# Score tiles of two heads in one TensorE tile: keys kept twice, key blocks not split over batches

## The chip, the cores and the metric

The kernel runs on one core of a Trainium2 chip. The metric is the device time of one execution in microseconds (us), before and after one change. The engines are TensorE (PE, with its weight loads shown as PEld), VectorE (DVE), ScalarE (ACT), GpSimd (POOL) and SyncE (SP), which only issues transfers here. Each engine works through its own queue in order and waits at semaphores for the others.

## What is computed

A parallel block: layer norm, then causal attention over a window of 256 tokens with 32 heads of 16 channels, and a gated bilinear feed-forward of width 1792, both added to the input. There are 2048 tokens of 512 channels; inputs and the output are bf16.

```python
xn = layernorm(x)                                   # x: (1, 2048, 512)
q, k, v = split(xn @ wqkv)                          # 32 heads, 16 channels each
scores = einsum("bhqd,bhkd->bhqk", q, k) * 16 ** -0.5
mask = (i - j >= 0) & (i - j < 256)                 # i: query, j: key
p = softmax(where(mask, scores, -1e9))
attention = merge_heads(einsum("bhqk,bhkd->bhqd", p, v)) @ wo
ffn = einsum("bsf,fd->bsd", (xn @ w_gate) * (xn @ w_up), w_down)
out = x + attention + ffn
```

## The kernel before

The tokens are cut into four chunks T of 512 tokens (eight blocks of 64), and the 32 heads into four groups c of eight heads. One of the 16 combinations (T, c) is called a pair; pairs run in the order of T and then c, and are numbered 0 to 15.

For a pair, the scores of keys against queries are taken in blocks of 64 keys by 64 queries. A query block q needs the key blocks q - 4 to q, so a pair of T 1 to 3 has 40 such blocks (each for eight heads) and a pair of T = 0 has 30. The function `layout` (L50) lists them by hand as batches of segments `(k, q, m, at)`: key block k (negative: of the chunk before) against m query blocks from q on, written at column block `at` of the score tile. A pair has five batches (four for T = 0), each up to eight column blocks wide. The eight heads of a group lie as four row strips of 32 partitions (index e); each strip holds two heads of 16 channels, called lanes. Keys are stored as K, and a second time as Ko, where the rows of the even head are set to zero (`i_odd`, L236). `i_scores` (L186) issues eight matmuls for a segment: for lane 0 16 rows of K, for lane 1 32 rows of Ko, each giving a tile of 64 keys by 64 m queries; lane 0 lands in PSUM partitions 0 to 63, lane 1 in 64 to 127, strip e in the e-th bank of the score tile S (four banks, one copy).

ScalarE takes the exponential of a whole batch from S into one of seven SBUF buffers P (L450). GpSimd then sets what the mask excludes to zero: `i_select` (L199, its instruction is L203) clears a triangle in diagonal blocks (q = k) and the other triangle in blocks q = k + 4. `selects` (L61) makes the list for one batch: it takes two blocks of the same kind into one instruction when their columns lie exactly four apart (a 64x512 select), and one alone otherwise (64x256); each is issued once per lane. The selects of one batch depend on each other in the planner's list. Then `i_values` (L206) multiplies with V, again eight matmuls for a segment, summed in two PSUM banks M; VectorE transposes, divides (L477, L486) and transposes back into OT.

PSUM has four more banks, M0 to M3, which the dense matmuls share (L184: q, k, gate, up, down, output projection; L595: v). VectorE and ScalarE evacuate them; on k this is `k_out` (L611).

The order of each engine's queue is made when the kernel is built, by a planner (`loop`, `choose`, `do`) that keeps estimated times of its own. A score batch can be placed once its keys, its queries, the score tile and a buffer P are free (`score_deps`); of seven buffers a pair holds five until its values are done, so at most two batches of the next pair can stand ahead of them. Batches are also kept at least `PACE` = 3.0 us apart in the planner's time. Values are placed when all selects of the pair should be done (`value_deps`); dense work fills the rest. Each operation carries the planner's estimate of its duration, such as 1.12 us for the values of a pair.

Of the kernel before, what the change touches and what calls it, by code (L numbers as in the profile page):

```python
# [8 lines left out]
F32 = mybir.dt.float32  # L9
I32 = mybir.dt.int32  # L10
ACT = mybir.ActivationFunctionType
ALU = mybir.AluOpType
# [37 lines left out]
def layout(T):  # L50


    ends = [(0, 4, 1, 0), (1, 5, 1, 1), (4, 4, 2, 2), (2, 6, 1, 4), (3, 7, 1, 5), (4, 6, 2, 6)]
    begins = [[(0, 0, 4, 0), (1, 1, 4, 4)], [(2, 2, 4, 0), (3, 3, 4, 4)]]
    if T == 0:
        return begins + [ends, [(5, 5, 3, 0), (7, 7, 1, 3), (6, 6, 2, 4)]]
    return [ends, [(-3, 0, 2, 0), (7, 7, 1, 2), (-2, 0, 3, 3), (6, 6, 2, 6)],
            [(-1, 0, 4, 0), (5, 5, 3, 4), (-4, 0, 1, 7)]] + begins
# [15 lines left out]
class Kernel:  # L74
# [11 lines left out]
    def open(self, ctx, tc, x, wqkv, wo, wg, wu, wd, out):  # L86
# [22 lines left out]
        self.K = some("K", 3, [128, 4, 512])  # L109
        self.Ko = some("Ko", 3, [128, 4, 512])  # L110
# [12 lines left out]
        self.odd = c.tile([128, 1], F32, name="odd")  # L123
# [4 lines left out]
    def prologue(self):  # L128
# [39 lines left out]
        nc.vector.tensor_copy(out=self.odd[:], in_=podd[:])  # L168
# [17 lines left out]
    def i_scores(self, T, c, batch):  # L186

        for k, q, m, at in batch:
            U, j = divmod(8 * T + k, 8)
            for lane in range(2):  # L190
                for e in range(4):
                    rows = slice(32 * e, 32 * e + (32 if lane else 16))
                    self.nc.tensor.matmul(  # L193
                        self.S[64 * lane:64 * lane + 64, e, 64 * at:64 * (at + m)],
                        lhsT=(self.Ko if lane else self.K)[U % 3][rows, c, 64 * j:64 * j + 64],
                        rhs=self.Q[T % 2][rows, c, 64 * q:64 * (q + m)],
                        start=True, stop=True, tile_position=(32 * e, 64 * lane), skip_group_check=True)
# [38 lines left out]
    def i_odd(self, T, c):  # L236
        self.nc.vector.tensor_scalar(out=self.Ko[T % 3][:, c, :], in0=self.K[T % 3][:, c, :],
                                     scalar1=self.odd[:, 0:1], scalar2=None, op0=ALU.mult)
# [186 lines left out]
    def score_deps(self, g):  # L425
        T, c, batch = self.batches[g]
        deps = {("S", g - 1), ("Pfree", g - self.PBUFS)}
        for k, q, m, at in batch:
            U, j = divmod(8 * T + k, 8)
            deps |= {("K", U, c, j // 2), ("Ko", U, c, j // 2), ("Q", T, c, q // 2), ("Q", T, c, (q + m - 1) // 2)}  # L430
# [30 lines left out]
    def do_values(self, at):  # L461
# [3 lines left out]
        o = self.pe(at, 1.12 if T else 0.86, f"V{v}")  # L465
# [57 lines left out]
    def first_chunk(self):  # L523
# [10 lines left out]
        first = []  # L534
        for b in range(4):
# [18 lines left out]
            def kq_out(o, i, b=b, tok=tok):  # L554
                x = self.op(f"K0b{b}", {"V": (0.21, 0.3)}, [o],
# [164 lines left out]
```

## Time and profile before

| | |
|---|---|
| time, median of 3 runs | 291.81 us (291.37 to 295.12) |
| time of the profiled execution | 291.58 us |
| its span, first to last instruction | 289.8 us |
| mean granted TensorE clock | 0.993 |
| instructions in the profile | 11641 |
| DMA traffic | 14.10 MB, mean 49 GB/s |

The 1.8 us between span and time lie outside the program's instructions. In the rows of the profile, "L203" is line 203 of the kernel; "P<-P" names what an instruction writes and reads; "64x512" is partitions by elements; "x208" is a count. In a group's row, the number after the bar is busy time in us, then the mean duration of one in ns, and after the second bar the idle time of the engine just before them with what ended it. In a row of a timeline the first two numbers are start and duration in us, and what stands in brackets is the idle time before it. In the chain in order of time they are the start of a piece and its length. In the table of windows there are, behind the window and its length, the busy times of PE, PEld, DVE, ACT and POOL with their counts, then the granted clock, the DMA share and GB/s.

### The profile page before, as it was taken

The page shows a single profiled execution, that of the slowest core. Times are in us where ns is not written, and L with a number is a line of the kernel's source. Part 1 is how long each engine was busy: PE and PEld are TensorE (multiplying, and loading weights), DVE is VectorE, ACT ScalarE, POOL GpSimd, SP SyncE. Part 2 cuts the span into 40 slices and gives each one's busy share as a digit, 9 for nine tenths or more (in the row PEclk, how much of TensorE's full clock was granted, in tenths as well). Part 3 has the DMA queues.
Part 4 walks back from the last instruction along what each step waited for, and adds up shares of the span by engine and source line. Part 5 has one row for each costly group of instructions (what it writes and reads, how often), then busy time and mean ns, then how long its engine had stood idle before and what let it go on. Part 6 is the DMA issues. An engine that isn't in the chain of part 4 may idle for free.

```text
span 289.8 us, 11641 instructions
## 1 busy us (share of the span) xinstructions
PE 271.8 (94%) x5296; PEld 138.5 (48%) x5296; DVE 185.0 (64%) x332; ACT 153.6 (53%) x98; POOL 175.5 (61%) x289
## 2 busy tenths in 40 slices
PE   6899999999999999798999899997997989989994
PEld 6564545665454545364454434546443444444541
DVE  7878987878954285767963466774614158658603
ACT  2057666567766656464856546652672735636000
POOL 3037695769868695658588664963657557484100
PEclk9999999999999999999999999999997999999999
DMA  7999310000041000000042000000000000000002
GB/s 228 374 370 351 81 20 2 3 5 2 2 76 38 23 20 3 2 2 5 0 78 57 20 2 2 2 3 5 2 18 23 18 23 2 1 5 2 2 0 72
DMA packets 17072, 14.10 MB, mean 49 GB/s; under 512 B 7040, under 2 KB 17024, under 8 KB 17024
## 3 DMA queue, kind: packets, MB, share of 16 engines
q1 hardware_dynamic: 16464, 12.85, 14.6%
q8 instruction: 41, 0.67, 1.0%
q10 hardware_dynamic: 560, 0.52, 0.6%
q14 instruction: 7, 0.06, 0.1%
HBM read 9.70 MB, written 2.10 MB: 41 GB/s over the span
## 4 chain that ended last, share of the span: by engine, by line
PE 81%; issue 7%; POOL 5%; DMA 2%; ACT 2%; SPq 1%; DVE 0%; ACTq 0%; POOLq 0%; DVEq 0%
PE M L184 60%; PE S L193 9%; PE M L213 7%; POOL P L203 5%; PE M L595 4%; DMA Wqkv<-in_A_wqkv_dram 2%; ACT P L450 2%; SPq L134 1%; DVE y L665 0%; DVE xnT L180 0%; DVE K L180 0%; ACTq L450 0%; POOLq L203 0%; DVEq L180 0%
## 5 line engine op out<-in xcount | busy, mean ns | idle before, releaser
L203 POOL TENSOR_SCALAR_AFFINE_SELECT P<-P 64x512 bf16<-64x512 bf16 (+1 forms) x272 | 169.0, 627 | 87.4 <-ACT P L450 75.5
L450 ACT ACTIVATE P<-S 128x2048 bf16<-128x2048 f32 x76 | 140.9, 1854 | 94.5 <-PE S L193 81.2
L184 PE MATMUL M<-xnT,Wg 128*128 128x512 bf16 x224 | 57.7, 380 | 0.0
L184 PE MATMUL M<-xnT,Wu 128*128 128x512 bf16 x224 | 57.7, 380 | 0.0
L184 PE MATMUL M<-Wd,hT 128*128 128x512 bf16 x224 | 54.7, 387 | 0.0
L644 DVE TENSOR_TENSOR hT<-M,gsb 128x512 bf16<-128x512 f32 x56 | 38.3, 683 | 12.9 <-PE M L184 12.4
L481 DVE STREAM_TRANSPOSE at<-M 128x512 f32<-128x512 f32 x32 | 21.4, 699 | 32.7 <-PE M L213 32.6
L213 PE MATMUL M<-P,V 64*17 64x64 bf16 (+3 forms) x2048 | 26.2, 228 | 9.7 <-POOL P L203 5.3
L180 DVE CAST gsb<-M 128x512 bf16<-128x512 f32 x43 | 29.5, 686 | 7.4 <-PE M L184 7.4
L193 PE MATMUL S<-Q,Ko 32*64 32x64 bf16 (+3 forms) x1024 | 34.2, 234 | 0.1
L193 PE MATMUL S<-Q,K 16*64 16x64 bf16 (+3 forms) x1024 | 33.8, 234 | 0.2 <-issue 0.2
L665 DVE TENSOR_TENSOR y<-M,x 128x512 bf16<-128x512 f32 x16 | 11.1, 692 | 35.8 <-PE M L184 35.6
L193 PEld LDWEIGHTS <-K 16*64 16x64 bf16 x1024 | 18.3, 104 | 31.9 <-issue 31.0
L184 PEld LDWEIGHTS <-hT 128*128 128x128 bf16 x224 | 20.3, 99 | 25.6 <-issue 4.3
L184 PEld LDWEIGHTS <-Wu 128*128 128x128 bf16 x224 | 20.5, 98 | 25.1 <-issue 2.2
L184 PE MATMUL M<-xnT,Wqkv 128*128 128x512 bf16 (+1 forms) x152 | 30.6, 346 | 2.1 <-DMA Wqkv<-in_A_wqkv_dram 0.9
L184 PEld LDWEIGHTS <-Wg 128*128 128x128 bf16 x224 | 20.0, 98 | 24.2 <-issue 2.0
L213 PEld LDWEIGHTS <-V 64*17 64x17 bf16 x2048 | 20.8, 84 | 13.3 <-issue 11.8
L184 PEld LDWEIGHTS <-Wqkv 128*128 128x128 bf16 x152 | 12.8, 98 | 15.7 <-issue 2.6
L193 PEld LDWEIGHTS <-Ko 32*64 32x64 bf16 x1024 | 17.7, 104 | 0.2 <-issue 0.2
L595 PE MATMUL M<-Wqkv,xnT 128*64 128x256 bf16 x256 | 15.5, 274 | 0.7 <-ACT xnT L178 0.7
L184 PE MATMUL M<-Wo,OT 128*128 128x512 bf16 x64 | 16.1, 379 | 0.0
(39 smaller groups left out, 143.9 us busy)
## 6 DMA issues: line engine op xcount, KB each, us to landing
out_dram<-y SPq DMA_DIRECT2D x16, 128.0 KB, 1.7
Wg<-in_B_w_gate_dram SPq DMA_DIRECT2D x2, 896.0 KB, 10.3
Wu<-in_B_w_up_dram SPq DMA_DIRECT2D x2, 896.0 KB, 11.9
Wd<-in_B_w_down_dram SPq DMA_DIRECT2D x1, 1792.0 KB, 17.6
Wqkv<-in_A_wqkv_dram SPq DMA_DIRECT2D x2, 512.0 KB, 6.4
x<-in_A_x_dram SPq DMA_DIRECT2D x1, 1024.0 KB, 13.5
x<-in_A_x_dram SPq DMA_DIRECT2D x1, 512.0 KB, 11.9
Wo<-in_A_wo_dram SPq DMA_DIRECT2D x1, 512.0 KB, 13.6
```

Source lines behind the costliest of these rows:

```text
L134: eng.dma_start(out=dst, in_=src)
L180: self.nc.vector.tensor_copy(out=out, in_=in_)
L184: self.nc.tensor.matmul(ps, lhsT=a, rhs=b, start=first and n == 0, stop=last and n == len(pairs) - 1)
L193: self.nc.tensor.matmul(self.S[64 * lane:64 * lane + 64, e, 64 * at:64 * (at + m)], lhsT=(self.Ko if lane else self.K)[U % 3][rows, c, 64 ...
L203: self.nc.gpsimd.affine_select(out=v, in_=v, pattern=[[0, 4], [0, n], [sign, 64]], base=0, fill=0.0, compare_op=ALU.is_gt if kind else ALU ...
L213: self.nc.tensor.matmul(banks[lane][32 * e:32 * e + 17, 64 * q:64 * (q + m)], lhsT=self.V[U % 3][rows, j, 4 * c + e, 0:17], rhs=P[rows, e, ...
L450: ex = self.op(f"exp{g}", {"A": (took + 0.06, took + 0.18)}, [o], lambda e: self.nc.scalar.activation(out=P[:, :, 0:hi], in_=self.S[:, :, ...
L481: t = self.op(f"tr{v}", {"V": (0.63, 0.71)}, [o] + ts, lambda e, par=par: nc.vector.transpose(out=self.at[:, :, par, :], in_=self.M[banks[ ...
L595: self.nc.tensor.matmul(self.M[i][64 * lane:64 * lane + 64, 256 * jj:256 * jj + 256], lhsT=self.xnT[T % 2][:, k, tok], rhs=w[:, lane], sta ...
L644: x = self.op(f"u{T}.{f}", {"V": PSUM_COPY["V"]}, [o, ("gate", T, f)], lambda e: self.nc.vector.tensor_tensor(out=self.hT[T % 2][:, f, :], ...
L665: self.nc.vector.tensor_tensor(out=keep["y"][:], in0=self.M[i][:], in1=self.x[:, t, :], op=ALU.add)
```

## The change

Keys are stored in one tile of shape [128, 4, 8, 2, 64]: for each group and key block two lanes of 64 keys, lane 0 with the odd head's rows zero, lane 1 with the even head's. One matmul with 32 rows and 128 key columns then gives the scores of both heads of a strip, so a segment takes four score matmuls. Each evacuation of keys becomes two operations that read the PSUM bank one after the other and multiply by a column of ones and zeros (`own`); the copy from K to Ko is gone.

The table in `layout` is new as well: a key block's segment, up to five query blocks, is never split over two batches. A pair has 12 segments in place of 17 (T = 0: 9 in place of 13), in as many batches. The planner's estimate for the values of a pair is raised.

```diff
 def layout(T):
-    ends = [(0, 4, 1, 0), (1, 5, 1, 1), (4, 4, 2, 2), (2, 6, 1, 4), (3, 7, 1, 5), (4, 6, 2, 6)]
...
-    return [ends, [(-3, 0, 2, 0), (7, 7, 1, 2), (-2, 0, 3, 3), (6, 6, 2, 6)],
...
+    return [[(3, 3, 5, 0), (-3, 0, 2, 5), (-4, 0, 1, 7)], [(2, 2, 5, 0), (6, 6, 2, 5), (7, 7, 1, 7)],
...
-        self.K = some("K", 3, [128, 4, 512])
-        self.Ko = some("Ko", 3, [128, 4, 512])
+        self.K = some("K", 3, [128, 4, 8, 2, 64])
...
-            for lane in range(2):
-                for e in range(4):
-                    rows = slice(32 * e, 32 * e + (32 if lane else 16))
-                    self.nc.tensor.matmul(
-                        self.S[64 * lane:64 * lane + 64, e, 64 * at:64 * (at + m)],
-                        lhsT=(self.Ko if lane else self.K)[U % 3][rows, c, 64 * j:64 * j + 64],
-                        rhs=self.Q[T % 2][rows, c, 64 * q:64 * (q + m)],
-                        start=True, stop=True, tile_position=(32 * e, 64 * lane), skip_group_check=True)
+            for e in range(4):
+                rows = slice(32 * e, 32 * e + 32)
+                self.nc.tensor.matmul(
+                    self.S[:, e, 64 * at:64 * (at + m)],
+                    lhsT=self.K[U % 3][rows, c, j].rearrange("p l t -> p (l t)"),
+                    rhs=self.Q[T % 2][rows, c, 64 * q:64 * (q + m)],
+                    start=True, stop=True, tile_position=(32 * e, 0), skip_group_check=True)
...
-    def i_odd(self, T, c):
-        self.nc.vector.tensor_scalar(out=self.Ko[T % 3][:, c, :], in0=self.K[T % 3][:, c, :],
-                                     scalar1=self.odd[:, 0:1], scalar2=None, op0=ALU.mult)
+    def i_keys(self, e, T, c, lane, in_, blocks=slice(0, 8)):
+
+        out, in_ = self.K[T % 3][:, c, blocks, lane, :], in_.rearrange("p (j t) -> p j t", t=64)
+        own = self.own[:, lane:lane + 1]
+        if e == "A":
+            self.nc.scalar.activation(out=out, in_=in_, func=ACT.Copy, scale=own)
+        else:
+            self.nc.vector.tensor_scalar(out=out, in0=in_, scalar1=own, scalar2=None, op0=ALU.mult)
...
-        o = self.pe(at, 1.12 if T else 0.86, f"V{v}")
+        o = self.pe(at, 1.42 if T else 1.12, f"V{v}")
...
         def k_out(o, i):
-            x = self.op(f"K{T}.{c}", PSUM_COPY, [o], lambda e: self.copy(e, self.K[T % 3][:, c, :], self.M[i][:]), rank=1)
+            x = o
+            for lane in range(2):
+                x = self.op(f"K{T}.{c}", PSUM_COPY, [o, x], lambda e, lane=lane: self.i_keys(
+                    e, T, c, lane, self.M[i][:]), rank=1)
             self.frees(x, i)
-            y = self.op(f"Ko{T}.{c}", {"V": (0.31, 0.44)}, [x], lambda e: self.i_odd(T, c), rank=4)
             for b in range(4):
-                self.at_["K", T, c, b], self.at_["Ko", T, c, b] = x, y
+                self.at_["K", T, c, b] = x
```

`selects` and `i_select` are not touched, but their lists follow from the table. GpSimd's queue at the start of a pair of chunk 3, before (pair 12: its first batch in buffer P_87, the next in P_88; "4x64" is one block for the four strips, "8x64" two blocks):

```order
L203 AFFINE_SELECT P_87<-P_87 64x4x64 [waits Activation_49]
L203 AFFINE_SELECT P_87<-P_87 64x4x64 [waits PE_49]
L203 AFFINE_SELECT P_87<-P_87 64x8x64 [waits PE_49,Pool_49] x2
L203 AFFINE_SELECT P_87<-P_87 64x8x64 x2
L203 AFFINE_SELECT P_88<-P_88 64x8x64 [waits Activation_49]
L203 AFFINE_SELECT P_88<-P_88 64x8x64 [waits PE_49]
```

and now (pair 13: its first batch in P_89, the next in P_90):

```order
L201 AFFINE_SELECT P_89<-P_89 64x4x64 [waits Activation_49]
L201 AFFINE_SELECT P_89<-P_89 64x4x64 [waits PE_49,Pool_49]
L201 AFFINE_SELECT P_89<-P_89 64x4x64 [waits Pool_49] x2
L201 AFFINE_SELECT P_89<-P_89 64x4x64 [waits PE_49] x2
L201 AFFINE_SELECT P_89<-P_89 64x4x64 [waits Pool_49]
L201 AFFINE_SELECT P_90<-P_90 64x4x64 [waits Activation_49]
```

The first batch of a pair had two one-block and four two-block selects; it now has eight one-block selects, the last of which stands behind the first select of the next batch.

The planner also orders TensorE's queue anew. At the values of pair 11, the last of chunk 2, before (scores of pair 12's first batch, then the first values):

```order
L193 LDWEIGHTS Ko_75
L193 MATMUL S<-Q_71,Ko_75 64x128
L213 LDWEIGHTS V_80
L213 MATMUL M_110<-P_89,V_80 17x64 [waits Pool_49]
L213 LDWEIGHTS V_80
L213 MATMUL M_110<-P_89,V_80 17x64
```

now, first the last dense matmuls ahead of these values (the up projection of chunk 2) and the first values,

```order
L183 LDWEIGHTS Wu
L183 MATMUL M_106<-xnT_78,Wu 128x512
L211 LDWEIGHTS V_77 [waits DVE_49]
L211 MATMUL M_107<-P_86,V_77 17x320 [waits Pool_49]
L211 LDWEIGHTS V_77
L211 MATMUL M_107<-P_86,V_77 17x320
```

and at their end the last values and the first matmuls behind them, for the keys of chunk 3 (then come its queries and a first part of its values, and then the scores of pair 12):

```order
L211 LDWEIGHTS V_77
L211 MATMUL M_108<-P_90,V_77 17x256
L183 LDWEIGHTS Wqkv [waits DMAHW2_49,DMAHW3_49,DMAHW1_49,DMAHW0_49]
L183 MATMUL M_109<-xnT_79,Wqkv 128x512 [waits DVE_49]
L183 LDWEIGHTS Wqkv
L183 MATMUL M_109<-xnT_79,Wqkv 128x512
```

The scores of pair 12's first batch, with the keys, queries and first values of chunk 3, have moved from ahead of pair 11's values to behind them. Between the scores of pair 12's last batch and those of pair 13's first there stand 52 dense matmuls now.

25 lines of the change are left out of this document (11 added, 14 removed).

## The prediction

> **What bounds the kernel now.** I read the page's list of engines first, then the chain that ended last, then the list of waits, then the chain in order of time.
>
> ```profile
> PE 271.8 (94%) x5296; PEld 138.5 (48%) x5296; DVE 185.0 (64%) x332; ACT 153.6 (53%) x98; POOL 175.5 (61%) x289
> PE 81%; issue 7%; POOL 5%; DMA 2%; ACT 2%; SPq 1%; DVE 0%; ACTq 0%; POOLq 0%; DVEq 0%
> PE M L213 <- POOL P L203: 5.3, 3, 2.1
> PE M L213 <- issue: 4.4, 3, 1.7
> ```
>
> TensorE (PE) sets the pace, and nearly its only waits are in the value matmuls of line 213, for the selects of GpSimd (POOL, line 203): 5.3 + 4.4 = 9.7 us. GpSimd has 114 us to spare. The next rows, the chain in order of time, show one pair: a batch of scores (S, L193), twelve dense matmuls (M, L184), and so on, then the values (M, L213).
>
> ```profile
> 104.78 0.35 PE S L193 x16
> 105.14 2.69 PE M L184 x12
> 107.83 0.35 PE S L193 x16
> 108.19 2.69 PE M L184 x12
> 110.88 0.53 PE S L193 x48
> 111.41 2.70 PE M L184 x12
> 114.11 0.36 PE S L193 x32
> 114.47 1.50 PE M L213 x121
> 115.97 1.47 issue
> ...
> 270.47 1.44 PE M L213 x123
> 271.90 14.15 PE M L184 x65
> 286.08 0.69 DVE y L665
> ```
>
> Dense matmuls come every 14.15 / 65 = 0.217 us. From 104.78 to 107.83 are 3.05 us with twelve of them (2.60), so a batch of 16 score matmuls costs 0.45 us. A batch of 48 takes 0.53 where 16 take 0.35 and 32 take 0.36: the matmuls of a batch overlap, and only the six-segment batch pays for its number of instructions.
>
> **The change on TensorE.** Segments fall from 17 to 12 in a pair (13 to 9 in token chunk 0), the score matmuls of a segment from eight to four. A batch now has two or three segments; the streamed columns are the same. So a batch costs 0.35 to 0.36, and what goes is the six-segment batch's 0.53 - 0.35 = 0.18, once in each of 16 pairs: 2.9 us. Values: 0.18 for four extra segments is 0.045 for one; some five fewer are 0.2 us for each of 16 pairs, 3.2 us (bounds: nothing, since the columns stay, and 5/17 of 1.44 us, 6.8 in all; I take 3.2, since short segments are what the score row prices). Together 6.1 us of TensorE time. Loads of 32x128 weights have no row. The nearest:
>
> ```profile
> 104.71 0.11 PEld L193 LDWEIGHTS <-K 16*64 16x64 bf16 x4 [0.42 <-issue]
> L184 PEld LDWEIGHTS <-Wu 128*128 128x128 bf16 x224 | 20.5, 98 | 25.1 <-issue 2.2
> ```
>
> Four loads of 64 columns take 0.11 us together, and one of 128 columns 0.098. So four of 128 lie between 0.11 (no change, which I take, since a full load is no longer than a small one) and twice that, some 0.25 us a batch, 1.8 us over the seven batches of steps 3 and 4 below.
>
> **The change on GpSimd.** It follows from the layout, and no line of the select itself changes. A select takes two blocks in one instruction only where they lie four columns of the table apart. The old table was laid out for that: a pair of chunks 1 to 3 has 14 two-block and 4 one-block selects (chunk 0: 10 and 4). In the new table segments of 5 and 3 put the diagonals five columns apart: 32 one-block selects a pair (chunk 0: 20, and 2 two-block). All in all 272 become 472.
>
> ```profile
> L203 POOL TENSOR_SCALAR_AFFINE_SELECT P<-P 64x512 bf16<-64x512 bf16 x208 | 139.8, 678 | 44.0 <-ACT P L450 34.3
> L203 POOL TENSOR_SCALAR_AFFINE_SELECT P<-P 64x256 bf16<-64x256 bf16 x64 | 29.5, 462 | 43.4 <-ACT P L450 41.2
> 200.01 0.98 POOL L203 TENSOR_SCALAR_AFFINE_SELECT P<-P 64x256 bf16<-64x256 bf16 x2 [4.53 <-ACT P L450]
> ```
>
> Half the work costs 462 ns against 678. The spacing is 0.98 - 0.462 = 0.518 where the second waits for the first (the timeline row), and 0.462 + (43.4 - 41.2) / 64 = 0.496 over the group. I take 0.51: in the new order over half of the selects carry a wait. Then GpSimd needs 32 x 0.51 = 16.3 us for a pair. TensorE needs, for a pair with 52 dense matmuls, 52 x 0.217 + 5 x 0.45 + 1.44 = 15.0. So GpSimd becomes the bound in chunks 1 to 3, and the saving on TensorE is spent in waiting at line 213.
>
> One more cost falls on GpSimd: a select that meets VectorE's multiply of line 486 takes far longer.
>
> ```profile
> 102.07 0.78 DVE L486 TENSOR_TENSOR on<-at,rz 128x512 bf16<-128x512 f32 x1
> 102.27 1.11 POOL L203 TENSOR_SCALAR_AFFINE_SELECT P<-P 64x512 bf16<-64x512 bf16 x1
> L203 POOL TENSOR_SCALAR_AFFINE_SELECT P<-P x272: 450/661/1150, 16.4 to 269.1; 64x512 bf16<-64x512 bf16 x106, 64x256 bf16<-64x256 bf16 x30
> ```
>
> 1.11 against a median of 0.66: 0.4 us, once a pair, and a GpSimd that is never idle cannot miss it. The Trainium skill's page GPSIMD Engine Reference (section 8, Key points) says that GpSimd shares its SBUF interfaces with VectorE and contends with VectorE instructions that have two SBUF inputs, as this multiply has; the trace agrees. Without that effect the sum below would be 4.4 us lower.
>
> **Keys.** Each evacuation of keys becomes two reads of the PSUM bank, and the copy Ko goes.
>
> ```profile
> L180 DVE CAST K<-M 128x512 bf16<-128x512 f32 x14 | 9.6, 689 | 2.4 <-PE M L184 2.2
> L237 DVE TENSOR_SCALAR Ko<-K,odd 128x512 bf16<-128x512 bf16 x16 | 6.9, 430 | 0.4
> ```
>
> On VectorE a chunk goes from 0.689 + 0.430 to 2 x 0.689, 0.26 us more for 15 chunks, on an engine that is 64% busy; a bank stays taken 0.7 us longer, one of four. The cover is VectorE's idle third; if it is gone at the first keys of chunk 3, up to 0.7 us on the path. I take nothing. The small preparation of the two columns of ones and zeros lies beside loads.
>
> **The sum, along the new path.** It rests on these rows.
>
> ```profile
> 14.02 0.35 PE S L193 x16
> 16.40 1.40 POOL L203 TENSOR_SCALAR_AFFINE_SELECT P<-P 64x512 bf16<-64x512 bf16 x2 [7.30 <-ACT P L450]
> 20.46 1.46 POOL L203 TENSOR_SCALAR_AFFINE_SELECT P<-P 64x512 bf16<-64x512 bf16 x2 [2.67 <-ACT P L450]
> L228 POOL TENSOR_TENSOR rs<-ve,mhalf 128x4 f32<-128x4 f32 x3 | 3.0, 1010 | 1.3 <-DVE ve L224 1.1
> 201.00 0.18 issue
> 201.18 0.39 PE M L213 x12
> 201.57 1.87 PE M L595 x32
> ```
>
> 1. Chunk 0 stays paced by scores. The first select starts at 16.4 as before; four pairs of 1.40 + 20 x 0.51 = 11.6 are 46.4; GpSimd waits 2.7 for the second batch, about 1 later, and one root takes 1.0: 67.5.
> 2. Pairs 4 to 11 without a gap: 8 x 16.3 = 130.6, two roots 2.0, eight multiplies 3.2: 203.3. There is no gap because, when a pair's last select ends, about 13 selects of the next two batches are queued, 6.6 us; the third batch, which needs the buffers that the values free, reaches GpSimd after 0.57 (end of the values, 201.00 to 201.57), about 1.0 of dense work and 2.4 (score to select, 14.02 to 16.40): 3.9.
> 3. At pair 11 the new order puts k, q and v of chunk 3 behind the values and ahead of the next scores, where before these scores stood ahead of the values. So GpSimd runs dry: 0.57 + 0.2 + 8 x 0.217 + half of 1.87 = 3.4, scores at 206.7.
> 4. From these scores to the first scores of pair 13, TensorE has 84 dense matmuls (18.2), 32 for v (1.87) and five batches (2.25): 229.0. GpSimd, done with pair 12 earlier, waits again; selects start 2.4 later, 231.4.
> 5. Pairs 13 to 15: 3 x 16.3 = 49.0, and three multiplies 1.2: 281.6.
> 6. The last values end 0.57 later; 44 dense matmuls remain, 9.5; from the last of them to the span's end is 289.8 - 271.9 - 65 x 0.217 = 3.8 as before: 295.5.
> 7. TensorE waits some 3 us before step 6. What such a wait does is in these rows.
>
> ```profile
> 220.89 0.62 PE L213 MATMUL M<-P,V 64*17 64x256 bf16 x16 [2.08 <-POOL P L203]
> 221.00:225.00 4.00, 4.00 (x49) 1.33 (x43) 3.07 (x5) 0.23 (x1) 1.73 (x3) 0.60 0.02 4
> ```
>
> After a wait of 2.08 us the granted clock was 0.60 over the next 4 us: 0.4 x 4, say 1.7 us. Added: a span of 297.2, 7.4 more than 289.8. The profiled run was 291.58, 1.8 over its span, and the median 291.81; so 297.2 + 2.0 = 299.2. The Trainium skill's page TensorE: Matmul & The Clock Gate (section Why this matters for your kernels) wants no idle gap over about 3 us; by it the wait of 3 us would lie at the limit and the time would be 297.5. The trace shows the loss after 2.08 already and decides.
>
> **The rivals.**
>
> A, faster: TensorE stays the bound, since selects come closer together. Then the waits of 9.7, the clock loss of 1.7 and the 6.1 go: 289.8 - 17.5 = 272.3, a time of 274. For it: TensorE's instructions do fall. Against it: a pair's selects would have to fit into 15.0 us, a spacing under 0.47, and the bare duration is 0.462.
>
> B, no difference: GpSimd is the bound, but its selects run at 0.496 and the multiply is met as seldom as now. Then up to 352 x 0.014 = 4.9 (the selects of steps 2 and 5) and 4.4 for the multiplies go: 299.2 - 9.3 = 289.9, and up to 297 where they go in part. For it: many of the new selects carry no wait.
>
> C, slower still: GpSimd runs dry after each pair, as the ring of seven buffers lets the third batch in only behind the values. It decides from the point at which 3.9 us of step 2 become more than 6.6, for which TensorE must lose 2.7 us there, at half clock and behind a late evacuation. One microsecond beyond at ten places is 10 us: 309. Against it: the margin.
>
> **How the numbers follow.** My forecast, 299.2, has 0.45; A 0.10; B 0.33; C 0.12. Two per cent, about what a measurement of this kernel can tell from no change, are 286.0 and 297.6. Slower: forecast and C, 0.57; same: B, 0.33; faster: A, 0.10. The range takes in the forecast with its slower loads (301.0), B from 289.9 on and half of C: 289 to 306.
>
> **What would show it.** Right: about 472 selects and GpSimd busy over 215 us, ninety per cent and more from 68 to 200; waits of line 213 for line 203 of 15 us or more, at nearly each pair from 4 on; two holes in GpSimd near 203 and 225; no score batch over 0.4 us. Wrong: a spacing under 0.49, values that find their selects done (A, B), or GpSimd idle after every pair (C).

## The result, and the profile after

The changed kernel takes 281.25 us (median of 4 runs, 280.19 to 284.13) against 291.59 for the kernel before (4 runs, 291.14 to 295.12): a ratio of 0.9635, 95% interval 0.9531 to 0.974. It is faster by 3.6%. The forecast was 299.2, slower, and the time lies below the range of 289 to 306. The profiled execution took 281.73 us, its span is 280.0. Ratios, here and below, compare only runs within 1.5% of the fastest of the same kernel.

The page of the changed kernel, with its engines, the chain that ended last, two groups (scores are line 191 now, values 211, selects 201), and one row of the list of waits:

```profile
PE 262.8 (94%) x3321; PEld 127.2 (45%) x3360; DVE 185.1 (66%) x331; ACT 156.0 (56%) x103; POOL 215.2 (77%) x489
PE 63%; POOL 25%; issue 3%; DMA 3%; ACT 2%; DVE 2%; SPq 1%; POOLq 0%; ACTq 0%; DVEq 0%
L201 POOL TENSOR_SCALAR_AFFINE_SELECT P<-P 64x256 bf16<-64x256 bf16 x464 | 203.6, 451 | 34.0 <-ACT P L453 15.3
L211 PE MATMUL M<-P,V 64*17 64x320 bf16 (+4 forms) x1440 | 24.1, 253 | 4.9 <-POOL P L201 3.0 <-DVE hT L645 1.1 <-DVE gsb L179 0.6
PE M L211 <- POOL P L201: 3.0, 8, 0.9
```

GpSimd is busy 215.2 us where it was 175.5, as forecast, and it holds 25% of the chain where it held 5%. But the value matmuls wait 4.9 us in all, where they waited 9.7 before and 15 or more were forecast, and TensorE's busy time falls by 9.0 us (of its 3360 matmuls 39 are missing from this trace, so a part of the 9.0 may be theirs). GpSimd's timeline gives its stretches without a gap (start, length, count):

```profile
81.74 89.76 POOL L201 TENSOR_SCALAR_AFFINE_SELECT P<-P 64x256 bf16<-64x256 bf16 x188
171.47 1.00 POOL L226 TENSOR_TENSOR rs<-ve,mhalf 128x4 f32<-128x4 f32 x1
172.45 17.74 POOL L201 TENSOR_SCALAR_AFFINE_SELECT P<-P 64x256 bf16<-64x256 bf16 x37
195.87 14.83 POOL L201 TENSOR_SCALAR_AFFINE_SELECT P<-P 64x256 bf16<-64x256 bf16 x32 [5.69 <-ACT P L453]
218.05 45.70 POOL L201 TENSOR_SCALAR_AFFINE_SELECT P<-P 64x256 bf16<-64x256 bf16 x96 [7.35 <-ACT P L453]
```

A select comes every 89.76 / 188 = 0.477 us, collisions with VectorE included: 15.3 us for the 32 of a pair, not 16.7 (16.3 and 0.4 for a multiply). The two holes of 5.69 and 7.35 us that the forecast had placed are there.

TensorE's timeline, cut where the first instruction behind three value groups starts, shows where the time went. The two columns on the right are runs told of below.

| stage (us) | before | after | old estimate | old estimate, no two-block select |
|---|---|---|---|---|
| to the end of the values of pair 3 | 72.0 | 69.2 | 70.7 | 70.6 |
| from there to the end of those of pair 11 | 129.5 | 121.4 | 122.7 | 117.5 |
| from there to the end of those of pair 15 | 70.3 | 74.4 | 63.2 | 63.2 |
| tail | 17.9 | 15.1 | 17.9 | 17.9 |
| span | 289.8 | 280.0 | 274.4 | 269.2 |

The middle stage gains 8.1 us; chunk 3 loses 4.0 and gets 2.9 back in the tail (from unrounded times). In the whole kernel the gain is thus cut down in one stage, and two questions are open: what was won in the middle, and what chunk 3 costs.

### The profile page after: what moved, and what is told of

Its sections match the earlier page's. It is cut to its first block, busy times and chain, and to the rows that moved or that the text cites. A ratio compares the mean times of both kernels' runs of the same rounds, so it can differ in the third digit from the quotient of the medians.

```text
span 280.0 us, 7936 instructions
## 1 busy us (share of the span) xinstructions
PE 262.8 (94%) x3321; PEld 127.2 (45%) x3360; DVE 185.1 (66%) x331; ACT 156.0 (56%) x103; POOL 215.2 (77%) x489
## 3 DMA queue, kind: packets, MB, share of 16 engines
q1 hardware_dynamic: 16464, 12.85, 15.3%
## 4 chain that ended last, share of the span: by engine, by line
PE 63%; POOL 25%; issue 3%; DMA 3%; ACT 2%; DVE 2%; SPq 1%; POOLq 0%; ACTq 0%; DVEq 0%
PE M L183 49%; POOL P L201 25%; PE S L191 6%; PE M L211 4%; PE M L594 4%; DMA Wqkv<-in_A_wqkv_dram 3%; ACT P L453 2%; POOL rs L226 1%; SPq L132 1%; DVE xn L231 0%; DVE at L484 0%; DVE y L666 0%; DVE gsb L179 0%; DVE hT L645 0%; POOLq L716 0%
## 5 line engine op out<-in xcount | busy, mean ns | idle before, releaser
L201 POOL TENSOR_SCALAR_AFFINE_SELECT P<-P 64x256 bf16<-64x256 bf16 (+1 forms) x472 | 208.7, 454 | 43.3 <-ACT P L453 24.3
L183 PE MATMUL M<-xnT,Wg 128*128 128x512 bf16 x213 | 56.6, 380 | 0.6 <-issue 0.2
L183 PE MATMUL M<-Wd,hT 128*128 128x512 bf16 x213 | 53.1, 389 | 2.0 <-issue 1.0
L179 DVE CAST gsb<-M 128x512 bf16<-128x512 f32 x44 | 30.3, 688 | 7.5 <-PE M L183 6.9
L191 PE MATMUL S<-Q,K 32*128 32x320 bf16 (+3 forms) x720 | 30.0, 254 | 0.9 <-ACT P L453 0.9
L211 PE MATMUL M<-P,V 64*17 64x320 bf16 (+4 forms) x1440 | 24.1, 253 | 4.9 <-POOL P L201 3.0
L191 PEld LDWEIGHTS <-K 32*128 32x128 bf16 x720 | 12.0, 92 | 32.9 <-issue 32.0
L241 DVE TENSOR_SCALAR K<-M,own 128x512 bf16<-128x512 f32 (+1 forms) x32 | 19.6, 646 | 5.0 <-PE M L183 4.8
L211 PEld LDWEIGHTS <-V 64*17 64x17 bf16 x1440 | 17.0, 85 | 10.4 <-issue 6.3
L183 PE MATMUL M<-Wo,OT 128*128 128x512 bf16 x64 | 16.3, 380 | 0.0
L594 PEld LDWEIGHTS <-xnT 128*64 128x64 bf16 x256 | 13.3, 110 | 2.7 <-issue 1.5
```

The lines of the kernel that those rows point to most:

```text
L179: self.nc.vector.tensor_copy(out=out, in_=in_)
L183: self.nc.tensor.matmul(ps, lhsT=a, rhs=b, start=first and n == 0, stop=last and n == len(pairs) - 1)
L191: self.nc.tensor.matmul(self.S[:, e, 64 * at:64 * (at + m)], lhsT=self.K[U % 3][rows, c, j].rearrange("p l t -> p (l t)"), rhs=self.Q[T % ...
L201: self.nc.gpsimd.affine_select(out=v, in_=v, pattern=[[0, 4], [0, n], [sign, 64]], base=0, fill=0.0, compare_op=ALU.is_gt if kind else ALU ...
L211: self.nc.tensor.matmul(banks[lane][32 * e:32 * e + 17, 64 * q:64 * (q + m)], lhsT=self.V[U % 3][rows, j, 4 * c + e, 0:17], rhs=P[rows, e, ...
L241: self.nc.vector.tensor_scalar(out=out, in0=in_, scalar1=own, scalar2=None, op0=ALU.mult)
```

## The experiments

All ran beside the kernel before on the same chip. A "wait" in a value group is a distance of over 0.4 us between the starts of two of its matmuls; sums of waits are worked out from the trace that way. The first four runs take the change apart. Some of the texts on record number value groups from 1: their group 7 is that of pair 6.

### Old estimate

The changed kernel, with the planner's estimate for the values put back.

```diff
-        o = self.pe(at, 1.42 if T else 1.12, f"V{v}")
+        o = self.pe(at, 1.12 if T else 0.86, f"V{v}")
```

> The changed kernel with the planner's estimate for the values of a pair back at 1.12 (0.86 for chunk 0), so that TensorE's queue keeps the order of the kernel before (pair 12's first scores ahead of pair 11's values). Theory P (price: the one-block selects cost about 0.465 from start to start, not 0.51, so GpSimd no longer sets the pace and TensorE's saving counts): the gain stays, 279 to 285 us, ratio 0.96 to 0.98. Theory O (order: the raised estimate places the values later and that is what took the waits at the value matmuls away): 287 us or more, ratio over 0.985, value matmuls waiting 11 us or more for selects.

Measured: 275.65 us (275.36 to 276.14), ratio 0.9406 (0.934 to 0.9472), lower than both theories had it. The holes of 5.69 and 7.35 us on GpSimd shrink to 0.81 and 0.16:

```profile
197.72 26.99 POOL L201 TENSOR_SCALAR_AFFINE_SELECT P<-P 64x256 bf16<-64x256 bf16 x57 [0.81 <-ACT P L453]
224.87 31.05 POOL L201 TENSOR_SCALAR_AFFINE_SELECT P<-P 64x256 bf16<-64x256 bf16 x64 [0.16 <-ACT P L453]
```

Chunk 3 takes 63.2 us instead of 74.4, and the tail takes back 2.8 of it. So the raised estimate, which moves dense work and the inputs of chunk 3 between pairs 11 and 13, costs 281.25 - 275.65 = 5.6 us, and the rest of the change gains 16 to 17.

### Single selects in the kernel before

No two-block selects, keys, tiles and table as before. This gives the kernel before the number of selects that the change brings.

```diff
-            if a - 4 in cols:
-                continue
-            out.append((kind, a, 2 if a + 4 in cols else 1, 4))
+            out.append((kind, a, 1, 4))
```

> The kernel before with its table, keys and tiles, but no two blocks in one select: 480 one-block selects, 32 a pair as in the changed kernel. Theory P: spacing 0.46 to 0.48 us in chunks 1 to 3, GpSimd busy 212 to 220 us, time within 2% of before (290 to 296), since 32 x 0.47 = 15.0 us is no more than TensorE needs for a pair here. The price of the prediction (0.51): 16.3 us a pair, eleven pairs 1 us or more longer, 300 us or more, ratio over 1.03.

Measured: 292.31 us (10 runs), ratio 0.9964 (0.9913 to 1.0016): nothing that can be told from no change.

```profile
PE 268.2 (92%) x5249; PEld 139.1 (48%) x5296; DVE 184.4 (64%) x334; ACT 152.4 (53%) x96; POOL 204.4 (70%) x497
L211 PE MATMUL M<-P,V 64*17 64x64 bf16 (+3 forms) x2048 | 25.6, 227 | 8.5 <-issue 6.6
```

GpSimd goes to 204.4 us busy, less than the 212 to 220 expected (the section on two-block selects shows why), and the waits in the value groups stay where they were, in the groups of pairs 6, 9, 11, 12 and 14, 1.8 to 2.1 us each; only that of pair 13 is gone. If these waits were for selects, 29 us more of selects would have made them longer. They had to have another cause.

### Tiles alone, and table alone

Tiles alone: keys and score tiles as in the change, but the table and estimate of before. Table alone: the kernel before with the new table. The core of each edit, the first against the changed kernel, the second against the kernel before:

```diff
...
-            [(0, 0, 5, 0), (5, 5, 3, 5)], [(1, 1, 5, 0), (-2, 0, 3, 5)], [(-1, 0, 4, 0), (4, 4, 4, 4)]]
+            [(-1, 0, 4, 0), (5, 5, 3, 4), (-4, 0, 1, 7)]] + begins
```

```diff
...
-    return [ends, [(-3, 0, 2, 0), (7, 7, 1, 2), (-2, 0, 3, 3), (6, 6, 2, 6)],
+    return [[(3, 3, 5, 0), (-3, 0, 2, 5), (-4, 0, 1, 7)], [(2, 2, 5, 0), (6, 6, 2, 5), (7, 7, 1, 7)],
...
```

> Keys kept twice and 32x128 score tiles with the old table and the old estimate: what the first half of the change does alone. Theory P: score matmuls 2048 to 1024, the six-segment batch from 0.53 to 0.36-0.42 us, 16 of them, so 2 to 4 us less: 288 to 290 us, ratio 0.985 to 0.995. If full 128-column loads run one after the other (the bound of the prediction): batches of 16 and 24 old matmuls get longer, 292 or more. Theory O: no gain at all, 291 to 293.

> The new table with the old keys and 32x64 tiles and the old estimate: the second half of the change alone, with 472 selects. Theory P: no six-segment batch (2.9 us less), 12 value segments for 17 (2 us less), selects at 0.46 to 0.48 us: 284 to 289 us, ratio 0.97 to 0.99. The price of the prediction (0.51): GpSimd the bound, 296 us or more. Theory O: 290 or more.

Measured: 276.74 us (ratio 0.9448, 0.9372 to 0.9523) for the tiles, 275.73 (ratio 0.9408, 0.9341 to 0.9475) for the table. Each alone gives 16 to 17 us, as much as both together with the old estimate, and several times what the expectations had. What they share is that they remove TensorE instructions: the whole queue has 10606 before, 8558 with the tiles, 8175 with the table and 6734 with both. And in both the long waits in the value groups are gone: none with the tiles, though their value groups still have 17 segments; with the table 2.8 us in pieces of under 0.9, for selects.

### What the waits were

The row of the kernel before that the prediction read as a wait for GpSimd is this one in GpSimd's timeline, around the values of pair 11 (197.87 to 201.50, waiting until 201.18):

```profile
194.09 1.39 POOL L203 TENSOR_SCALAR_AFFINE_SELECT P<-P 64x512 bf16<-64x512 bf16 x2 [1.66 <-ACT P L450]
200.01 2.43 POOL L203 TENSOR_SCALAR_AFFINE_SELECT P<-P 64x256 bf16<-64x256 bf16 x4 [4.53 <-ACT P L450]
```

GpSimd was idle from 195.48 to 200.01. The last select of pair 11 was done 2.4 us before its values began; those at 200.01 are of the next pair. So it is everywhere in the kernel before: by the order of the queues, the last select of each of the 16 pairs ended 0.6 to 3.0 us before its values began. What did happen in the wait is in the table of transfers for 198 to 199 us (forty slices, so of 0.025 us each):

```profile
DMA  0000000000000000000000900000000000000000
...
q8 instruction: 1, 0.02, 7.2%
```

One packet of 16 KB on the queue that brings instructions, at 198.55, in a kernel that otherwise transfers nothing here. The 10606 instructions of TensorE come with 41 such packets, the 8558, 8175 and 6734 of the runs above with 33, 32 and 26: 256 in each. In the kernel before each of the six long waits has such a packet 0.1 to 1.1 us ahead of it. A value group of chunks 1 to 3 is 272 instructions in 1.44 us, the densest stretch of the kernel. Hence a theory: TensorE's supply of instructions runs dry in a value group that lies badly to the 256s. The Trainium skill's page Runtime: NRT & Kernel Launch (section Instruction fetch mechanics) says that the instruction memory is refilled in blocks of 16 KiB, 256 instructions, and that this is mostly hidden.

### Shifting the instructions by 128 and by 192

The place of the value groups in the 256s can be moved with nothing else: some gate and up blocks of chunk 0 are computed in two halves of 256 columns (`f < 8` in the first run, `f < 12` in the second). The planner's order and the selects stay.

```diff
-            self.matmuls(self.M[i][:], [(W[:, k, 128 * f:128 * f + 128], self.xnT[T % 2][:, k, :]) for k in range(4)])
+            halves = 2 if T == 0 and f < 8 else 1
+            w = 512 // halves
+            for h in range(halves):
+                self.matmuls(self.M[i][:, w * h:w * h + w],
+                             [(W[:, k, 128 * f:128 * f + 128], self.xnT[T % 2][:, k, w * h:w * h + w]) for k in range(4)])
```

> The kernel before with one edit: 8 gate and 8 up blocks of chunk 0 are computed as two 128x256 halves instead of one 128x512 block, which puts 128 more TensorE instructions ahead of the seventh value group and changes neither the planner's order nor any select. Supply theory (TensorE's instructions come in 256s, and a value group of 272 short ones that starts late in such a stretch runs dry): the starts of the value groups move by half a stretch, from places 182, 184, 202, 210, 10 and 242 of 256 for the six that stood still to 54, 56, 74, 82, 138 and 114, and only the eleventh (now at 200) lies where the stalled ones lay. So waits of 1.5 to 2.4 us inside groups 7, 10, 12, 13, 14 and 15 go, one may come in group 11, their sum falls from 11.2 to about 2 us, and the time falls by 7 to 10 us to 283 to 286. Select theory (the groups wait for GpSimd's selects): the same six groups stand still as before, the time stays at 292.8 plus at most 0.5 us for the extra matmuls.

> The same edit on 12 gate and 12 up blocks: 192 more TensorE instructions. Supply theory: places 118, 120, 138, 146 for groups 7, 10, 12, 13 (free), 202 for group 14, 178 for group 15 (at the edge), and 234, 236 and 8 for groups 6, 9 and 11, which had none before and now get one: 4 or 5 waits of 1.5 to 2.4 us, in other groups than before, sum 6 to 10 us, time 287 to 293. Select theory: groups 7, 10, 12, 13, 14, 15 stand still as before, 6, 9 and 11 do not, time 293.

Measured: 286.11 us with 128 (4 runs, 282.83 to 287.65; ratio 0.9768, 0.9665 to 0.9872), 291.69 with 192 (ratio 0.99, 0.9774 to 1.0026). The place of a group's first instruction in its 256, counted in the program, and the wait inside the group in us, from the trace:

```
pair       4    5    6    7    8    9    10   11   12   13   14   15
before     166  42   182  168  44   184  72   202  210  10   242  216
  wait     -    -    1.74 -    -    1.92 -    2.13 2.35 1.51 1.50 -
+128       38   170  54   40   172  56   200  74   82   138  114  88
  wait     -    -    -    -    -    -    1.88 -    -    -    -    -
+192       102  234  118  104  236  120  8    138  146  202  178  152
  wait     -    1.42 -    -    2.71 -    -    -    -    1.94 -    -
```

The waits go where the places say, to groups that had none, and leave those that had them. With 128 the group of pair 11 runs through and that of pair 10 stands still, in the chain in order of time:

```profile
179.76 0.36 PE S L193 x32
180.12 1.38 PE M L213 x112
181.50 1.61 issue
183.11 0.39 PE M L213 x11
...
197.21 0.53 PE S L193 x48
197.74 1.51 PE M L213 x124
```

The run with 192 can't be told from no change; of the four executions with 128 the profiled one (282.83 us) is the fastest. The spans are 289.8 us before, 281.2 with 128, where 9.3 us of waits in groups are gone, and 288.7 with 192, where 5.1 are gone; there chunk 0 takes 2.3 us longer, and waits of 0.5 and 1.4 us stand in the dense work. Groups at places 182 to 242 stood still in these three kernels, but for 216 in pair 15, the one with no packet near it; one at 10 did too, while one at 8 did not. In the run with single selects the group of pair 13 had moved to 98, and ran through.

The traces say it more sharply than the starts of the groups. Take every stretch of over 0.4 us in which TensorE runs neither a matmul nor a weight load, without the first 14 and the last 8 us, and count its instructions up to it by the weight loads and semaphore instructions in the trace. In the kernel before, with single selects, with the two shifts and with tiles alone (shifted or not, the former told of below) there are 26, in value groups, scores and dense work, and all 26 begin when one and the same place of the 256 is reached, 196 in the count of the table. At each, the packet had started 0.2 to 1.4 us after this place was passed the time before, and TensorE went on 2.2 to 3.0 us after the packet's start. In all 13 kernels the place is never passed less than 2.2 us after the start of its packet (taking the n-th packet with the n-th passing, 394 in all). A group that begins at 182 has 270 of its instructions ahead of this place, one at 10 has 186, and they take 1 to 1.5 us: the packet comes too late.

A wait for a select looks different: in the runs whose value groups wait for selects (those with the new table and two-block selects), such a wait ends 0.05 us after the end of a select, at places without a pattern. The waits in the groups of the kernel before end 0.16 to 3.3 us after the select last done.

At 168 to 172 a wait of 1.1 to 1.7 us comes just behind the group, in the dense work: place 196 is 8 to 12 instructions behind these groups. The longest wait of all, 2.71 us in pair 8 with 192, fell on transposes of the activations. The table of transfers from 150 to 151 us:

```profile
DMA packets 499, 0.14 MB, mean 139 GB/s; under 512 B 498, under 2 KB 498, under 8 KB 498
...
q1 hardware_dynamic: 498, 0.12, 162.1%
q8 instruction: 1, 0.02, 5.8%
```

The packet itself took 0.93 us, no longer than at the other 25 waits (0.88 to 1.45), and TensorE went on 2.66 us after its start, as elsewhere. But it started 1.4 us after the place was passed before, the latest of all; whether the 498 others held it back is not shown. So the waits of 9.7 us in the kernel before are the supply of TensorE's instructions. Here the Trainium skill's page named above and the measurement differ: the fetch is not hidden in a stretch of 272 instructions in 1.44 us.

### Tiles alone, shifted by 64

This tells whether the tiles alone gained by their number of instructions or by a lucky place; the edit is the one above with `f < 4`, on the kernel with the tiles alone.

> The new tiles and keys with the old cut into segments and the old planner estimate (276.7 us, value groups still of 272 instructions, no wait in any), plus the halves on 4 gate and 4 up blocks: 64 more instructions. Groups 8 to 12 move from places 152, 148, 152, 160 and 154 of 256 to 216, 212, 216, 224 and 218. If the place alone decides, 5 waits of 1.5 to 2.4 us come, the sum 8 to 11 us, time 282 to 287: the tiles alone would then have gained nothing but a lucky place. If the fewer instructions ahead of a group (half as many for its scores) are what keeps the supply ahead, no wait comes and the time stays at 276.5 to 277.5.

Measured: 276.57 us (ratio 0.9478, 0.9393 to 0.9562), the same as without the shift (276.74). The groups of pairs 7 to 10 now lie at 216, 212, 216 and 224 and run through; only that of pair 11, at 218, waits, 1.82 us. In the four that run through, the packet had started 1.4 to 2.2 us before place 196 was passed the time before; in that of pair 11, 0.8 us after it. So the tiles did not gain by a lucky place: with half the score matmuls ahead of a group the supply is mostly far enough ahead, though not safe by much. The table alone was not shifted; its value groups have 192 instructions in place of 272.

### Selects one behind the other

The changed kernel with the old estimate; the planner is made to keep the selects of one batch together, where it mixes them with those of the next batch. By this TensorE's queue is reordered too (in chunk 0, for one, the values of each pair now come ahead of a batch of scores that they followed), so the order of the selects is not the only difference.

```diff
-                last = self.op(f"sel{g}", {"G": (cost, cost + 0.05)}, [ex, last],
-                               lambda e, m=m, lane=lane: self.i_select(P, lane, *m), rank=1)
+                last = self.op(f"sel{g}", {"G": (cost, cost - LAT)}, [ex, last],
+                               lambda e, m=m, lane=lane: self.i_select(P, lane, *m), rank=0.1 + 0.001 * g)
```

> The changed kernel with the old estimate (275.65 us), the selects of one score batch kept one behind the other instead of mixed with those of the next batch. Spacing theory (a select behind one on the same buffer starts 0.06 us late, behind one on another buffer at once): the spacing of one-block selects in chunks 1 to 3 goes from 0.465 to about 0.495 us, GpSimd needs 15.8 us a pair against TensorE's 15.0, value groups wait more for selects, time 278 to 284. Rival (the gap belongs to the lane or the kind of the select, not to the buffer): spacing and time stay within 0.5% of 275.65.

Measured: 289.88 us (10 runs, ratio 0.9914, 0.9867 to 0.9961), 14.2 us slower than with the mixed order, more than was expected. Stretches without a gap in GpSimd's timeline, first of the mixed order, then of the contiguous one:

```profile
78.38 64.58 POOL L201 TENSOR_SCALAR_AFFINE_SELECT P<-P 64x256 bf16<-64x256 bf16 x134
```

```profile
84.25 65.97 POOL L201 TENSOR_SCALAR_AFFINE_SELECT P<-P 64x256 bf16<-64x256 bf16 x129
PE M L211 <- POOL P L201: 9.4, 19, 2.3
```

The spacing goes from 64.58 / 134 = 0.482 to 65.97 / 129 = 0.511 us, the value the prediction took; the second row, from the list of waits, has the value groups waiting 9.4 us for selects, against 2.8. GpSimd works with no gap over 0.1 us from 84.25 to 207.02 us, so in chunks 1 and 2 its spacing sets the pace, whatever TensorE's order. 384 selects 0.029 us further apart are 11 us of the 14.2; TensorE also ran at half clock for 3.4 us twice (granted 0.51 over 153.5 to 157.0 and 235.4 to 238.9), some 3.4 us more. Per neighbours of one-block selects (spacings over 0.7 us left out), mean duration, mean gap behind it and spacing in ns:

```
                          next in same buffer     next in another buffer
changed kernel            441 + 59 = 500 (149)    438 + 13 = 451 (295)
old estimate              443 + 60 = 503 (171)    438 + 15 = 453 (275)
contiguous                442 + 61 = 504 (379)    426 + 68 = 494 ( 65)
kernel before             461 + 64 = 525 ( 53)    465 + 19 = 484 ( 10)
```

A select whose predecessor works on the same buffer starts 0.06 us after it; on another buffer, and with no wait of its own, at once. In the contiguous order all 65 that change the buffer carry a wait, and the gap is as long. In the kernel before nearly all neighbours are on the same buffer, so its rows hardly show the short spacing.

### Two-block selects and the comparison

In the kernel with the old estimate the selects that keep q >= k take 0.453 to 0.462 us and the others, with >, 0.417 to 0.424. First both were written with >, the former with a base of 1. Then, with the comparisons as they were, the eight two-block selects of chunk 0 were written as 16 of one block, by the edit of the second experiment.

```diff
-        self.nc.gpsimd.affine_select(out=v, in_=v, pattern=[[0, 4], [0, n], [sign, 64]], base=0, fill=0.0,
-                                     compare_op=ALU.is_gt if kind else ALU.is_ge, channel_multiplier=-sign)
+        self.nc.gpsimd.affine_select(out=v, in_=v, pattern=[[0, 4], [0, n], [sign, 64]], base=1 - kind, fill=0.0,
+                                     compare_op=ALU.is_gt, channel_multiplier=-sign)
```

> The changed kernel with the old estimate (275.65 us), both kinds of select written with the same comparison: the kind that keeps q >= k now asks q - k + 1 > 0. In that kernel the selects with >= took 0.453 to 0.462 us and those with > 0.417 to 0.424; in the kernel with single selects and the old keys both took 0.42. If the comparison sets the duration, all go to 0.42, GpSimd is busy some 8 us less (240 selects times 0.037), the spacing falls from 0.472 to about 0.455, and the time to 272 to 275, since GpSimd and TensorE are both near their bound. If it is something else (the two-block selects of chunk 0, which only that other kernel lacks), the durations stay at 0.455 and the time at 275.6.

> The changed kernel with the old estimate, the 8 two-block selects of chunk 0 written as 16 of one block; comparisons as they are. If the presence of a two-block select is what makes the one-block ones with >= take 0.455 instead of 0.42, all go to 0.42 and the time falls by 1 to 4 us, less 8 selects times 0.25 = 2 us of GpSimd in chunk 0, hidden there or not. If the comparison sets it, they stay at 0.455 and the time stays within 1 us of 275.65.

Measured: 282.32 us with one comparison (ratio 0.9679, 0.9611 to 0.9746), slower by 6.7, which neither side of its expectation had; 271.46 without two-block selects (ratio 0.9301, 0.9237 to 0.9365), faster by 4.2. With > alone the one-block selects take 0.455 to 0.461 (medians by kind and lane), with no two-block select 0.415 to 0.422, whatever the comparison; so it was in the second experiment too. The comparison with which a two-block select stands in the program is the slow one, also for the one-block selects, and 8 of 472 suffice. GpSimd's longest stretch, first with one comparison, then without two-block selects, the latter with its value matmuls and its chain:

```profile
78.51 66.87 POOL L201 TENSOR_SCALAR_AFFINE_SELECT P<-P 64x256 bf16<-64x256 bf16 x134
```

```profile
76.64 62.01 POOL L199 TENSOR_SCALAR_AFFINE_SELECT P<-P 64x256 bf16<-64x256 bf16 x134
L209 PE MATMUL M<-P,V 64*17 64x320 bf16 (+4 forms) x1440 | 21.1, 252 | 0.0
PE 93%; DMA 3%; issue 1%; SPq 1%; DVE 1%; DVEq 0%
```

At 62.01 / 134 = 0.463 us GpSimd needs 14.8 us a pair and drops out of the chain: no value group waits at all. The four kernels with the new tiles, the new table and the old estimate order themselves by spacing: 0.463 gives 271.5 us, 0.482 gives 275.7, 0.499 gives 282.3 and 0.511 gives 289.9. In the same order the eight pairs of chunks 1 and 2 take 14.7, 15.3, 15.9 and 16.7 us each, and 32 spacings are 14.8, 15.4, 16.0 and 16.4. TensorE alone thus needs at most 14.7 us for a pair, where the forecast had 15.0; with selects more than about 0.46 us apart GpSimd is the bound.

### The change without two-block selects

```diff
-            if a - 4 in cols:
-                continue
-            out.append((kind, a, 2 if a + 4 in cols else 1, 4))
+            out.append((kind, a, 1, 4))
```

> The changed kernel itself (raised estimate kept, 281.25 us), the 8 two-block selects of chunk 0 written as 16 of one block. The planned order is the same. If the selects' spacing and the place of the dense work are separate costs: all one-block selects take 0.42, the waits of the value groups (6.0 us) go nearly all, and the time falls by 3 to 5 us to 276 to 278; the two holes on GpSimd in chunk 2 stay (5.7 and 7.4 us, or longer by what GpSimd gains), so it stays 5 to 6 us above the 271.5 of the same kernel with the old estimate. If the holes only cost because GpSimd was slow, both estimates give the same time, 271 to 273.

Measured: 274.86 us (ratio 0.9383, 0.9345 to 0.9421), 6.4 less than the change itself, more than expected, and 3.4 above the 271.46 of the old estimate. The holes stay and are longer, as GpSimd's timeline shows:

```profile
192.98 14.21 POOL L199 TENSOR_SCALAR_AFFINE_SELECT P<-P 64x256 bf16<-64x256 bf16 x32 [6.20 <-ACT P L451]
215.16 14.55 POOL L199 TENSOR_SCALAR_AFFINE_SELECT P<-P 64x256 bf16<-64x256 bf16 x32 [7.97 <-ACT P L451]
```

The raised estimate costs 5.6 us where GpSimd is the bound and 3.4 where it isn't: partly separate, partly the same cost. The best version is the changed kernel with the old estimate and single selects: 271.46 us, 7.0% under the kernel before and 3.5% under the change.

## Why the prediction was wrong

**The step that failed: "GpSimd needs 32 x 0.51 = 16.3 us for a pair", in steps 2 and 5 of the sum.** The mechanism was right and the term too large: a pair took 15.3 us with the multiplies in it, where 16.7 were forecast. Set against the timeline, in us:

| step | forecast | measured |
|---|---|---|
| selects of pairs 4 to 11 end | 203.3 | 190.2 |
| from there to the first scores of pair 12 | 3.4 | 3.3 |
| from there to the first scores of pair 13 | 22.3 | 22.2 |
| from there to the first select of pair 13 | 2.4 | 2.4 |
| selects of pairs 13 to 15 | 50.2 | 45.7 |
| from their end to the end of the span, clock included | 15.6 | 16.3 |

The measured column is from GpSimd's rows shown above and these of the chain in order of time (the start of the first scores of pairs 12 and 13, and the tail):

```profile
193.46 0.33 PE S L191 x12
...
215.64 0.33 PE S L191 x12
...
263.81 0.34 PE M L211 x8
...
265.37 10.93 PE M L183 x42
```

All but two rows hold within 0.7 us. Those two are off by 13.1 and 4.5, together 17.6 where the span missed by 17.2; the others give some 0.4 back. Of the 13.1, 12.8 are step 2: chunk 0's selects ended, by the order of the queue, at 67.2 us, where step 1 has 67.5, and the eight pairs behind them took 123.0 us, where 135.8 were forecast. The spacing of 0.477 is under the 0.49 that the prediction named as its sign of being wrong. Both ends of the spacing, 0.518 and 0.496, came from neighbours that nearly all work on the same buffer. The order printed ahead of the prediction shows the selects of two batches mixed, and two thirds of the neighbours in the changed kernel are on different buffers. A lower end that allowed for no gap at all would have been the bare 0.462, and the forecast with it 32 x 0.048 x 11 = 17 us shorter.

**The diagnosis of the waits before was wrong too.** That TensorE's "nearly only waits are in the value matmuls of line 213, for the selects of GpSimd" rested on the releaser that the list of waits names, and on 4.4 us of "issue" counted as the same thing. GpSimd's own timeline contradicts it, and all these waits begin at one place of the 256 instructions. This did not enter the sum, since the path was laid through GpSimd, but it hid the largest gain: with these waits gone and the spacing short, each half of the change is worth 16 to 17 us.

**The terms on TensorE.** Values: with 17 segments and no wait they are busy 24.4 us (tiles alone), with 12 and no wait 21.1 (no two-block select), a gain of 3.3 where 3.2 was taken. The row of line 209 stands above, that of line 212 is:

```profile
L212 PE MATMUL M<-P,V 64*17 64x64 bf16 (+3 forms) x2048 | 24.4, 227 | 0.0
```

Score batches take 0.33 us each, none over 0.4, as forecast; over the kernel they cost 30.1 us before and 25.8 after (from the start of each batch to that of the next group), 4.3 less where 2.9 was taken. The loads of 32x128 weights cost nothing that shows, as taken.

**The multiplies.** The longest select is 0.99 us. Spacings over 0.7 us left out, the mean is 0.468, with them 0.477: 32 x 0.009 = 0.3 us a pair, 0.4 was taken.

**Keys at nothing.** VectorE's full evacuations of keys, two per bank as forecast, take 0.75 us each, where 0.69 was taken:

```profile
L241 DVE TENSOR_SCALAR K<-M,own 128x512 bf16<-128x512 f32 x24 | 17.1, 747 | 3.9 <-PE M L183 3.7
```

Line 211 waits 0.6 us for VectorE's `gsb` and 1.1 for its `hT` in the changed kernel; whether the second evacuation makes these late was not tried.

**The clock.** 1.7 us were taken, for a wait of 3 us. The windows at the end of the values have 0.57 over 4 us, which is 1.7 us; the wait before it was not one of 3 us but three of 0.5 to 0.74, so that the cost came out right is partly luck:

```profile
258.00:265.00 7.00, 5.04 (x111) 2.43 (x111) 0.83 (x2) 0.49 (x1) 5.43 (x14) 1.00 0.01 2
265.00:269.00 4.00, 3.95 (x11) 1.41 (x11) 2.25 (x4) 0.00 (x0) 0.00 (x0) 0.57 0.00 0
```

**The rivals.** None came as it was told. A had its condition nearly met (a spacing under 0.47; it was 0.477 with the collisions, and GpSimd stayed a quarter of the chain), and its 274 us is near what the change gives once the holes are gone (275.65). It was given 0.10, because the bare duration of 0.462 was taken as the least a spacing can be; where buffers alternate it is 0.451, gap included. B went the right way and stopped at 0.496.

## What to carry to other kernels

Where a list of waits names a releaser that had long been done, or "issue", look at that engine's own timeline and at the transfers in the same microseconds before an engine is blamed; if it is the supply of instructions, the waits begin at one place of the 256, and a shift that changes nothing else moves them. A kernel in which TensorE runs 272 instructions in 1.44 us can gain from fewer instructions by more than their own time. Before a spacing is taken from rows, ask whether the neighbours in those rows are of the kind that the new order will have.

## What the runs showed of the hardware

- TensorE's instructions came in packets of 16 KB, 256 at a time (41 packets for 10606 instructions). In 13 kernels a fixed place of each 256 was never passed less than 2.2 us after the start of its packet, and a burst of 272 in 1.44 us that reached the place with 186 or more of them behind it stood still there for 1.4 to 2.7 us, unless the packet had started early enough.
- GpSimd's one-block selects on two alternating buffers were spaced 0.45 us, on one buffer 0.50.
- One-block selects took 0.42 us in a program without two-block selects, and 0.455 for a comparison that also had two-block ones. Why, no run here shows.
- The granted clock fell to half (0.50 from 265.4 to 268.8 us) after three short waits of TensorE within 3 us, with no single long one. In the changed kernel's TensorE timeline the brackets hold the waits ahead of the window at 0.57:

```profile
262.59 0.26 PE L211 MATMUL M<-P,V 64*17 64x192 bf16 x4 [0.50 <-POOL P L201]
263.43 0.77 PE L211 MATMUL M<-P,V 64*17 64x192 bf16 x20 [0.58 <-POOL P L201]
264.94 1.02 PE L183 MATMUL M<-Wd,hT 128*128 128x512 bf16 x2 [0.74 <-DVE at L484]
```
